# Thresholded attention with a leaky two-layer projection: the weights of period 3 turned by TensorE in five pieces, and a score bank for the second layer of the last group but one

## The chip, the cores and the metric

The kernel runs on one core of a Trainium2 chip. The metric is the device time of one execution in microseconds. Its engines have their own instruction queues and run beside each other: TensorE (PE; its loads of stationary operands are listed as PEld), VectorE (DVE), ScalarE (ACT), GpSimd (POOL), and SyncE (SP), which here mainly issues DMA transfers. TensorE writes only to PSUM, which has eight banks of 2 KB a partition; ScalarE and VectorE take the results out.

## The reference

Eight batches of eight heads, 576 tokens of 64 values each. Every row of scores keeps what lies within tau (0.02) of the row's maximum, takes a softmax over that, and weights v. The result, as 4608 tokens of 512 values, goes through two dense layers with a leaky ReLU between them.

```python
scores = scale * np.matmul(q, k.transpose(0, 1, 3, 2))
thresh = np.max(scores, axis=-1, keepdims=True) - tau
scores = np.where(scores >= thresh, scores, -1000000000.0)
...
attn = np.exp(scores)
attn = attn / (np.sum(attn, axis=-1, keepdims=True) + 1e-09)
return np.matmul(attn, v).astype(np.float32)
...
h = x @ w_in
g = np.maximum(0.01 * h, h)
return (g @ w_out).astype(np.float32)
```

## The kernel before

**Periods.** The work is cut into 72 periods, n = 0 to 71. A main period takes 128 queries of one batch in four heads (two pairs): 8 batches x 4 blocks of queries x 2 halves of the heads. Eight more, the tails, take the last 64 tokens of a batch in all heads. The loop over n (L653) writes the instructions of every engine out by hand in the order in which they are to run; nothing is reordered later. An engine runs its queue in order, and the tile framework puts semaphores where one engine needs another's result or a buffer.

**What one period does.** At step n TensorE computes the scores of period n (L297) into one PSUM tile, `sc`, of five banks (2560 columns). VectorE copies four tiles of 128x576 out of it with their row minima (L338) and derives the thresholds (L356). ScalarE takes exponentials (L367), and VectorE multiplies them with the mask (L378); for the remaining tiles ScalarE does mask and exponential itself (L372, L373). That makes the weights `w` of period n, 128 queries x 18 blocks of 128 keys.

**Turning the weights.** The weighted sum needs the weights with the keys on the partitions. For periods 0 to 2 TensorE turns them against an identity, each block in two halves of 64 columns (`turn_w_here`, L399), into PSUM, and ScalarE or VectorE copies them into `wT` (`take_w`, L404); for periods from 3 on SP issues one DMA that transposes all 18 blocks (`turn_w`, L391), at step n + 1. SP's queue also carries the loads of q, k and v and the stores, in the order of the code.

**Weighted sum and layers.** Two steps later (PV_LAG), TensorE multiplies the turned weights with v (`pv`, L434); VectorE scales the result by the reciprocals of the sums, which TensorE has spread over the partitions (L414) and ScalarE copied to `by` (L420), and writes it to `x` (L453). Two main periods make a group of 128 tokens; its first layer is four pieces (`layer1`, L474, evicted by ScalarE at L477 to `g`), its second layer eight steps (`layer2`, L507), two of them at a time, eight matmuls in all. The result is evicted by ScalarE (L511) and stored by SP. At each step two such pieces of older groups are mixed in, one in each half of the step.

**Loads of the next batch.** q and k are split into halves of 16 bits by POOL, turned by TensorE (`turn`, L186) and copied to `kT` and `qT` (L249). At the first batch and for some pieces of the second, TensorE turns the 32-bit values instead (`turn32`, L211), with ScalarE (L232) and VectorE (L239) taking the two halves out; what `late32` lists for a step is such a piece. POOL loads `w_in` and `w_out` in eight pieces at steps 1 and 4.

**PSUM.** Five banks are `sc`; two more rotate under the tag "h" (turned q and k, turned weights, spread reciprocals, `pv`, the first layer's `hp`); one has the tag "o" (the second layer's sum; at early steps turned weights). The last two periods' `pv`, and the last group's second layer (`layer2_last`, L486), use columns of `sc`, since no scores come after.

Of the kernel before, what the change touches and what calls it, by code (L numbers as in the profile page):

```python
# [9 lines left out]
FP32 = mybir.dt.float32  # L10
FP16 = mybir.dt.float16
# [22 lines left out]
def kernel(  # L34
# [139 lines left out]
    def turn(keys):  # L174

        banks = [ps.tile([128, 1024], FP16, tag="h", bufs=2, name="tp") for _ in range(2)][::-1]
        at_ = 0
        for key in keys:
            half, n = halves.pop(key), tokens(key)
            tps[key] = [t[:, ds(at_, 128 * n)].rearrange("d (x t p) -> d x t p", x=2, t=n) for t in banks]  # L180
            at_ += 128 * n
            for x in range(2):
                for t in range(n):
                    for r in range(2):
                        rows = ds(64 * r, 64)
                        nc.tensor.transpose(tps[key][r][:, x, t, :], half[rows, x, t, :, :].rearrange("p h d -> p (h d)"),  # L186
                                            ident[rows, rows])
        return banks[0]


    def unit32(b, which, p0, np=1, t0=0, nt=4):
# [150 lines left out]
    def copies(st, before, taken, lows):  # L342
        taken()
        if st.n:
            copy_min(st, 1)
            copy_min(st, 2)
        if lows:
            take_low(lows[0])
        if not st.n:
            copy_min(st, 2)  # L350
        copy_min(st, 3)
        for keys in lows[1:]:
            take_low(keys)
        if before:
            recip(before)
        nc.vector.tensor_scalar(out=st.th[:, :], in0=st.mn[:, :], scalar1=1.0, scalar2=tau_f, op0=AX.mult, op1=AX.add)  # L356
        st.w = sb.tile([128, 2, 9, 128], FP16, tag="w", bufs=3, name="w")
        st.sum = sb.tile([128, 2, 2], FP32, tag="sum", bufs=3, name="sum")
# [36 lines left out]
    def turn_w_here(st, first, n, o):  # L395

        for i in range(n):
            for j in range(2):
                nc.tensor.transpose(o[ds(64 * j, 64), ts(i, 128)],  # L399
                                    st.w[:, :, :, :].rearrange("q c n d -> q (c n) d")[:, first + i, ds(64 * j, 64)],  # L400
                                    ident[:, :])

    def take_w(st, first, n, o, copy):
        return copy(out=st.wt[:, :, :, :].rearrange("k c n q -> k (c n) q")[:, ds(first, n), :],  # L404
                    in_=o.rearrange("k (n q) -> k n q", q=128))
# [12 lines left out]
    def take_spread(st, bank):  # L418
        st.by = sb.tile([128, 2, 128], FP16, tag="by", bufs=2, name="by")
        nc.scalar.copy(out=st.by[:, :, :], in_=bank[:, 768:1024].rearrange("d (c q) -> d c q", c=2))  # L420
# [78 lines left out]
    def layer2():  # L499
        g, r = l2q.pop(0)  # L500
        if g.where == (B - 1, 3):
            return layer2_last(g, r)
        if r == 0:
            g.o = ps.tile([128, 512], FP32, tag="o", bufs=1, name="o")
        for j in (2 * r, 2 * r + 1):
            for c in range(2):
                nc.tensor.matmul(out=g.o[ds(64 * c, 64), :], lhsT=g.g[:, j, ds(64 * c, 64)],  # L507
                                 rhs=w_out16[:, j, :], start=(j == 0), stop=(j == 15), skip_group_check=True)
        if r == 7:
            g.out = sb.tile([128, 512], FP32, tag="osb", bufs=3, name="osb")  # L510
            nc.scalar.activation(out=g.out[:, :], in_=g.o[:, :], func=AF.Copy, bias=0.0, scale=1.0)  # L511
            stores.append(g)
# [140 lines left out]
    while n < N + PV_LAG or l1q or pending or l2q or stores:  # L653
        st = periods[n] if n < N else None
        before = periods[n - 1] if 1 <= n <= N else None
        due = periods[n - PV_LAG] if PV_LAG <= n < N + PV_LAG else None
        here = before and before.n < 3
        rest = due and due.n < 3
        plain = 2 if n < 2 or n == 4 else 3
        keys, now32, late = turns_at.get(n, []), early32.get(n, []), late32.get(n)  # L660


        if n == 0:
            def between():
                copy_min(st, 0)
                copy_min(st, 1)
                take_low(k32[1])
                for x in now32:
                    turn32(x)
            scores(st, between)  # L670
            turn32(late)
        elif st:
            scores(st)
        if rest:
            o = ps.tile([128, 1024], FP16, tag="o", bufs=1, name="wp")
            turn_w_here(due, 12, 6, o[:, 0:768])
        bank = turn(keys) if keys else None
        for x in now32 if n else []:
            turn32(x)
        if here:  # L680
            before.wt = sb.tile([128, 2, 9, 128], FP16, tag="wT", bufs=4, name="wT")
            bank = ps.tile([128, 1024], FP16, tag="h", bufs=2, name="tp")
        if due:
            bank = spread(due, bank)
        if here:
            turn_w_here(before, 0, 6, bank[:, 0:768])
        for key in keys:
            take(key, 0, on_act)
        if due:
            take_spread(due, bank)  # L690
        for x in now32:
            take_high(x)
        if here:
            take_w(before, 0, 6, bank[:, 0:768], on_act)
        if st:
            def taken():
                for key in keys:
                    take(key, 1, on_dve)
                if rest:
                    take_w(due, 12, 6, o[:, 0:768], on_dve)  # L700
            copies(st, before, taken, now32)
            exp_plain(st, 0)
            if n == 0:
                exp_plain(st, 1)
                take_high(late)
                take_low(late)
        elif before:
            recip(before)
        work = [lambda key=key: split_pool(key) for key in split_at_.get(n, [])] + pool_at.get(n, [])
        for i, f in enumerate(work):  # L710
            mm = f()
            if i == 0 and before:
                behind_masks(mm, before)
        for key in keys:
            if key[1:] == ("t", "k"):
                widen_keys(key[0])
        if n >= 5:

            for f in small_at.get(n, []):
                f(small=nc.gpsimd)  # L720
        if n < 4:
            idle((4, 10, 8, 4)[n], spare("o"))
        if here:
            o = ps.tile([128, 1024], FP16, tag="o", bufs=1, name="wp")
            if n < 3:
                turn_w_here(before, 6, 6, o[:, 0:768])
        elif before:
            turn_w(before, 1 if st else 2)
        for f in loads_at.get(n, []) + (small_at.get(n, []) if n < 5 else []):
            f()  # L730
        while stores and (n >= N or n not in loads_at or len(stores) > 1):
            store()

        if due and n == 3:
            pv(due)
        if n == 3:
            turn32(late)
            turn_w_here(before, 6, 6, o[:, 0:768])
        for half in range(2):
            if half == 1 and n in (3, 4):  # L740
                exp_steep(st, plain)
            for _ in range(2):
                if l2q:
                    layer2()
            if l1q:
                layer1()
            elif n >= N:
                settle()
            if half == 0:
                if st:  # L750
                    for i in range(1, plain if n else 0):
                        exp_plain(st, i)
                        if n == 3 and i == 1:
                            take_high(late)
                if here:
                    take_w(before, 6, 6, o[:, 0:768], on_act)
                if late and n not in (0, 3):
                    turn32(late)
                    take_high(late)
                if due:  # L760
                    if n != 3:
                        pv(due)
                    evacuate(due)
            elif st and n != 3:
                for i in range(plain + (n == 4), 4):
                    exp_steep(st, i)
        if n == 4:
            take_low(late)
        for i in range(plain if st else 0):
            weights(st, i)  # L770
            if late and n != 4 and n and i == 0:
                take_low(late)
        n += 1
# [33 lines left out]
```

## Time and profile before

| what | value |
|---|---|
| three runs | 477.99, 480.15 and 481.57 us |
| median | 480.15 us |
| profiled execution | 480.22 us |
| its span, first to last instruction | 478.4 us |
| mean granted TensorE clock | 0.996 |
| busy in the span: PE, DVE, ACT, POOL | 462.8, 431.6, 419.1, 216.2 us |
| DMA moved | 84.26 MB, mean 176 GB/s |

A row of the timeline or of the chain begins with the start and the duration in microseconds after the span's start, then engine, line, operation, tiles (out<-in) and how many instructions are merged in it. Brackets at the end give the idle time of the engine before the row and what ended it. Durations of neighbours overlap by some 0.1 us, since the engines pipeline. In the busy time by stretches there follow, after the stretch and its length, the busy time of PE, PEld, DVE, ACT and POOL with their instructions, the granted clock of TensorE, the share of the DMA engines and GB/s. The chain of waits is followed back from the last instruction, at each step to what released it.

### The profile page before, as it was taken

To read this page: it belongs to the slowest core of one execution; us is meant where nothing else is said; L and a number is where in the kernel's file an instruction comes from. 1 tells how busy PE (TensorE), PEld (TensorE's weight loads), DVE (VectorE), ACT (ScalarE), POOL (GpSimd) and SP (SyncE) were. 2 spreads that over 40 slices of the span, in tenths; PEclk is the share of its full clock that TensorE was granted. 3 is DMA by queue.
4 is the path that set the end of the run, shared out by engine and by line. 5 is a ranking of instruction groups with operands and counts; after the bars stand their busy time and mean duration, and the time that the engine had idled before them with its cause. 6 is when DMAs were issued, how large, how long until landed. Compare 5 with 4: busy or idle time off the path is not lost.

```text
span 478.4 us, 25135 instructions
## 1 busy us (share of the span) xinstructions
PE 462.8 (97%) x10806; PEld 377.2 (79%) x10806; DVE 431.6 (90%) x1307; ACT 419.1 (88%) x782; POOL 216.2 (45%) x355
## 2 busy tenths in 40 slices
PE   6889889999999999999999999999999999999997
PEld 4667768888888888888888888888888888877776
DVE  3999969999999999999999999999999999999950
ACT  4898968999999999999999998999999999988862
POOL 2645646554465474455465574545357474000000
PEclk9999989999999999999999999999999999999999
DMA  9999998698899968799889987779889996765561
GB/s 174 236 218 195 188 225 164 156 204 178 201 162 192 246 147 210 117 188 203 186 185 182 210 187 176 150 181 202 189 190 173 200 214 129 117 131 124 123 146 46
DMA packets 208767, 84.26 MB, mean 176 GB/s; under 512 B 177648, under 2 KB 203504, under 8 KB 208656
## 3 DMA queue, kind: packets, MB, share of 16 engines
q1 hardware_dynamic: 201616, 75.25, 79.6%
q0 software_dynamic: 5568, 6.95, 7.7%
q8 instruction: 84, 1.38, 1.2%
q10 hardware_dynamic: 1472, 0.46, 0.4%
q14 instruction: 27, 0.22, 0.2%
HBM read 36.70 MB, written 9.44 MB: 96 GB/s over the span
## 4 chain that ended last, share of the span: by engine, by line
PE 87%; DVE 5%; DMA 4%; ACT 2%; issue 1%; SPq 0%; DVEq 0%; ACTq 0%
PE hp L474 25%; PE o L507 24%; PE sc L297 22%; PE pv L434 8%; DMA wT<-w 3%; PE tp L414 3%; PE tp L186 3%; DVE s L338 3%; DMA raw<-in_k_dram 1%; DVE w L378 1%; PE sc L486 1%; ACT g L477 0%; ACT s L372 0%; SPq L86 0%; ACT e L367 0%
## 5 line engine op out<-in xcount | busy, mean ns | idle before, releaser
L338 DVE TENSOR_SCALAR_CACHE_REDUCE s<-sc 128x576 f32<-128x576 f32 x288 | 205.5, 753 | 18.0 <-PE sc L297 17.9
L474 PEld LDWEIGHTS <-win 128*64 128x64 f16 x4608 | 147.1, 110 | 28.8 <-issue 1.3
L378 DVE SCALAR_TENSOR_TENSOR w<-s,th,e 128x576 f16<-128x576 f32 x213 | 163.6, 815 | 0.2
L367 ACT ACTIVATE e<-s,mn 128x576 f16<-128x576 f32 x213 | 157.8, 778 | 0.0
L507 PE MATMUL o<-wout,g 128*64 128x512 f16 x1120 | 145.0, 380 | 0.6 <-ACT osb L511 0.6
L474 PE MATMUL hp<-x,win 128*64 128x128 f16 x4096 | 137.1, 220 | 0.6 <-DVE x L453 0.3
L477 ACT ACTIVATE g<-hp 128x512 f16<-128x512 f32 x144 | 86.1, 598 | 42.8 <-PE hp L474 42.8
L297 PE MATMUL sc<-kT,qT 64*128 64x384 f16 (+7 forms) x1920 | 120.5, 284 | 2.2 <-DVE s L338 1.3
L297 PEld LDWEIGHTS <-qT 64*128 64x128 f16 (+1 forms) x1920 | 90.7, 97 | 18.6 <-issue 2.2
L160 POOL TENSOR_SCALAR scaled<-raw 128x512 f32<-128x512 f32 x53 | 32.7, 616 | 142.3 <-DVE w L378 129.5
L507 PEld LDWEIGHTS <-g 128*64 128x64 f16 x1120 | 56.8, 110 | 28.5 <-issue 0.7
L171 POOL TENSOR_TENSOR half<-scaled,half 128x512 f16<-128x512 f32 (+1 forms) x68 | 71.7, 1054 | 5.8
L373 ACT ACTIVATE w<-s,minus_tau 128x576 f16<-128x576 f32 x75 | 58.2, 775 | 2.4
L372 ACT ACTIVATE s<-s,th 128x576 f32<-128x576 f32 x75 | 57.5, 767 | 0.7 <-DVE th L356 0.7
L434 PE MATMUL pv<-wT,v 128*64 128x128 f16 (+1 forms) x1560 | 51.6, 214 | 3.7 <-DMA wT<-w 2.7
L434 PEld LDWEIGHTS <-v 128*64 128x64 f16 x1600 | 45.7, 110 | 5.1 <-DMA wT<-w 2.7
L167 POOL CAST half<-scaled 128x512 f16<-128x512 f32 (+1 forms) x68 | 38.3, 563 | 4.4
L453 DVE TENSOR_TENSOR x<-pv,by 128x256 f16<-128x256 f32 x62 | 26.3, 423 | 4.3 <-PE pv L434 4.2
L420 ACT COPY by<-tp 128x256 f16<-128x256 f16 x71 | 26.4, 372 | 0.0
L186 PEld LDWEIGHTS <-half 64*128 64x128 f16 x968 | 24.3, 95 | 2.6 <-issue 1.7
L186 PE MATMUL tp<-ident,half 64*128 64x64 f16 x968 | 24.2, 190 | 0.4 <-issue 0.4
L113 POOL CAST v<-vraw 128x256 f16<-128x256 f32 x64 | 24.5, 417 | 0.0
(64 smaller groups left out, 338.5 us busy)
## 6 DMA issues: line engine op xcount, KB each, us to landing
vraw<-in_v_dram SPq DMA_DIRECT2D x16, 512.0 KB, 5.5
out_dram<-osb SPq DMA_DIRECT2D x31, 256.0 KB, 3.9
raw<-in_q_dram SPq DMA_DIRECT2D x13, 512.0 KB, 4.8
raw<-in_k_dram SPq DMA_DIRECT2D x13, 512.0 KB, 5.5
win<-in_moe_w_in_dram POOLq DMA_DIRECT2D x4, 512.0 KB, 10.6
wout<-in_moe_w_out_dram POOLq DMA_DIRECT2D x4, 512.0 KB, 12.4
raw<-in_q_dram SPq DMA_DIRECT2D x12, 128.0 KB, 3.8
raw<-in_k_dram SPq DMA_DIRECT2D x10, 128.0 KB, 4.4
```

The source lines that it names most:

```text
L171: nc.gpsimd.tensor_tensor(out=halves[key][:, 1, 0:n, :, :], in0=scaled.pop(key)[:, 0:n, :, :], in1=halves[key][:, 0, 0:n, :, :], op=AX.sub ...
L186: nc.tensor.transpose(tps[key][r][:, x, t, :], half[rows, x, t, :, :].rearrange("p h d -> p (h d)"), ident[rows, rows])
L297: yield nc.tensor.matmul(out=o, lhsT=lhs, rhs=turned[st.b, "k"][rows, kx, pair, ds(key0, n)], start=(i == 0), stop=(i == 2), skip_group_ch ...
L338: return nc.vector.tensor_scalar(out=st.s[TILES[n]][:, :], in0=sc[:, ds(PLACE[TILES[n]], 576)], scalar1=-1.0 / UNIT, scalar2=None, op0=AX. ...
L367: nc.scalar.activation(out=st.e[t][:, :], in_=st.s[t][:, :], func=AF.Exp, bias=st.mn[:, n : n + 1], scale=-1.0)
L372: nc.scalar.activation(out=z, in_=z, func=AF.Prelu, bias=st.th[:, n : n + 1], scale=-1.0, alpha=1e20)
L373: nc.scalar.activation(out=w_of(st, t), in_=z, func=AF.Exp, bias=minus_tau[:, :], scale=1.0, accum_out=st.sum[:, c, h : h + 1])
L378: st.last = nc.vector.scalar_tensor_tensor(out=w_of(st, t), in0=st.s[t][:, :], scalar=st.th[:, n : n + 1], in1=st.e[t][:, :], op0=AX.is_le ...
L434: nc.tensor.matmul(out=st.pv[ds(64 * h, 64), c, ts(u, n)], lhsT=v16[st.b % 2][:, pair, blk, :], rhs=st.wt[:, c, blk - (blk > 4), ts(u, n)] ...
L474: nc.tensor.matmul(out=hp[ds(64 * c, 64), jj, :], lhsT=w_in16[:, i, ds(128 * (4 * u + jj) + 64 * c, 64)], rhs=g.x[:, i, :], start=(i == 0) ...
L477: nc.scalar.activation(out=g.g[:, ds(4 * u, 4), :], in_=hp[:, :, :], func=AF.Prelu, bias=0.0, scale=1.0, alpha=0.01)
L507: nc.tensor.matmul(out=g.o[ds(64 * c, 64), :], lhsT=g.g[:, j, ds(64 * c, 64)], rhs=w_out16[:, j, :], start=(j == 0), stop=(j == 15), skip_ ...
```

## The change

Two things are changed. First, the weights of period 3 are turned by TensorE instead of by a DMA from SP, in five pieces of 2, 2, 8, 4 and 2 blocks. At step 4, four blocks go in places that are free in banks already in use ("o" beside the rest of period 2's weights, and the bank of the turned k), and eight in a bank of their own under "o", between the first layer's piece and the late turn of q; at step 5, six go beside the turned q. ScalarE copies three pieces (2, 8 and 2 blocks), VectorE two (2 and 4). At step 4, the late q is turned and its high half copied before, not behind, ScalarE's second exponential. `turn` returns both its banks for this. Second, the second layer of the last group but one, (7, 2), sums in columns 512 to 1024 of `sc` instead of in "o".

```diff
-        return banks[0]
+        return banks
...
-            g.o = ps.tile([128, 512], FP32, tag="o", bufs=1, name="o")
+            g.o = sc[:, 512:1024] if g.where == (B - 1, 2) else ps.tile([128, 512], FP32, tag="o", bufs=1, name="o")
...
-        bank = turn(keys) if keys else None
+        if n == 4:
+            before.wt = sb.tile([128, 2, 9, 128], FP16, tag="wT", bufs=4, name="wT")
+            turn_w_here(before, 0, 2, o[:, 768:1024])
+        bank, side = turn(keys) if keys else (None, None)
...
+        if n == 4:
+            turn_w_here(before, 2, 2, bank[:, 512:768])
+        if n == 5:
+            turn_w_here(due, 12, 4, side[:, 512:1024])
+            turn_w_here(due, 16, 2, bank[:, 512:768])
         if due:
             bank = spread(due, bank)
...
             take_spread(due, bank)
+        if n in (4, 5):
+            take_w(periods[3], (2, 16)[n - 4], 2, bank[:, 512:768], on_act)
...
                 if rest:
                     take_w(due, 12, 6, o[:, 0:768], on_dve)
+                if n == 4:
+                    take_w(before, 0, 2, o[:, 768:1024], on_dve)
+                if n == 5:
+                    take_w(due, 12, 4, side[:, 512:1024], on_dve)
...
-        elif before:
+        elif before and n != 4:
             turn_w(before, 1 if st else 2)
...
             if half == 0:
+                if n == 4:
+                    o = ps.tile([128, 1024], FP16, tag="o", bufs=1, name="wp")
+                    turn_w_here(before, 4, 8, o[:, :])
+                    take_w(before, 4, 8, o[:, :], on_act)
+                    turn32(late)
+                    take_high(late)
...
-                if late and n not in (0, 3):
+                if late and n not in (0, 3, 4):
                     turn32(late)
                     take_high(late)
```

## The prediction

> **What bounds the kernel now.** I read the profile's page first: the clock of TensorE in 40 slices of 12 us, and the chain of work that ended last.
>
> ```profile
> PEclk9999989999999999999999999999999999999999
> ...
> PE 87%; DVE 5%; DMA 4%; ACT 2%; issue 1%; SPq 0%; DVEq 0%; ACTq 0%
> ```
>
> TensorE carries 87% of the chain, so a delay or a gain near the start is mostly carried to the end unchanged. Its clock drops below 9 tenths in one slice, the sixth (59.8 to 71.8 us). I went there with TensorE's timeline, then with the chain in order of time.
>
> ```profile
> 61.50 0.75 PE L434 MATMUL pv<-wT,v 128*64 128x128 f16 x20 [2.42 <-DMA wT<-w]
> ```
>
> ```profile
> 53.09 8.37 DMA wT<-w
> ...
> 62.25 1.19 PE o L507 x8
> 63.43 1.71 PE hp L474 x32
> 65.14 2.05 PE sc L297 x19
> ...
> 71.00 0.86 PE o L507 x8
> 71.87 0.89 PE hp L474 x32
> 72.76 1.65 PE sc L297 x20
> ```
>
> TensorE stands still for 2.42 us (59.08 to 61.50), until the turned weights of period 5 have landed at 53.09 + 8.37 = 61.46. What follows is slow: 1.19 where the same eight matmuls later take 0.86, 1.71 for 0.89, 2.05 for 1.65, together 0.33 + 0.82 + 0.40 = 1.55 us. The busy time by stretches has the reason in the column after the five engines, the granted clock:
>
> ```profile
> 63.00:64.00 1.00, 1.00 (x20) 0.78 (x16) 1.00 (x3) 0.00 (x0) 0.00 (x0) 0.50 1.43 244
> ```
>
> So this stall costs 2.42 + 1.55 = 3.97 us. Why the weights are late stands in SP's queue:
>
> ```profile
> 34.91 3.98 SPq L391 DMA_TRANSPOSE wT<-w  x1
> 39.00 0.50 SPq L75 DMA_DIRECT2D raw<-in_k_dram  x1
> 42.86 7.12 SPq L391 DMA_TRANSPOSE wT<-w  x1
> 50.08 2.90 SPq L86 DMA_DIRECT2D raw<-in_q_dram  x4
> 53.09 3.28 SPq L391 DMA_TRANSPOSE wT<-w  x1
> ```
>
> The three transposes are those of periods 3, 4 and 5, each issued one period later. From 42.86 to 53.09 the queue never rests, so period 5's is issued when SP comes to it. The change takes the first of the three out.
>
> **What periods 4 and 5 pay.** The weights are 18 blocks, so 36 half transposes on TensorE, with copies on ScalarE (256, 1024 and 256 columns) and VectorE (256 and 512). Prices come from turns that exist already: L399 on TensorE (twelve halves in a row of the first fence below) and L404 on ScalarE.
>
> ```profile
> 29.52 0.63 PE L543 MATMUL spare<-blank,ident 128*64 128x256 f16 x8 [0.97 <-DVE wT L404]
> 29.95 0.75 PE L434 MATMUL pv<-wT,v 128*64 128x128 f16 x20
> 30.63 0.65 PE L211 MATMUL tp<-ident,raw 128*128 128x128 f32 x4
> 31.22 0.53 PE L399 MATMUL wp<-ident,w 128*64 128x128 f16 x12
> ```
>
> ```profile
> 36.29 1.08 PE L474 MATMUL hp<-x,win 128*64 128x128 f16 x32 [0.28 <-DVE kT L249]
> ...
> 38.12 0.75 PE L434 MATMUL pv<-wT,v 128*64 128x128 f16 x20 [0.16 <-ACT g L477]
> ```
>
> ```profile
> 32.48 0.79 ACT L404 COPY wT<-wp 128x768 f16<-128x768 f16 x1
> 33.16 0.79 ACT L372 ACTIVATE s<-s,th 128x576 f32<-128x576 f32 x1
> ...
> 36.53 0.38 ACT L420 COPY by<-tp 128x256 f16<-128x256 f16 x1
> ```
>
> Twelve halves take 0.53 us, so one takes 0.044. Period 4 adds 24 of them, 1.06 us. Eight stand ahead of the projection at 36.29; its wait of 0.28 for VectorE swallows 0.17, since only the first four delay what VectorE waits for. The other sixteen stand between that projection and the weighted sum at 38.12, and swallow its wait of 0.16 for ScalarE. That leaves 1.06 - 0.17 - 0.16 = 0.73. Then comes a new wait: the second layer's bank ("o") has held those sixteen halves, and ScalarE copies them out only after it has evicted hp. Its copy of 768 columns runs 0.68 us from start to start (32.48 to 33.16), so 1024 take 0.90. That eviction releases the weighted sum at 38.12 today; behind the new first copy it ends near 38.55, the 1024 columns near 39.45, and TensorE comes for the bank at about the same moment. I put 0.07. Period 4 is 0.80 us later, period 5 another 12 x 0.044 = 0.53. Together 1.33.
>
> ScalarE's side gives the same: 256 columns last 0.38, 0.27 to the next start by the same overlap of 0.11, so its three copies add 0.27 + 0.90 + 0.27 = 1.44, and in period 5 the weighted sum waits for its eviction of hp. The two delays run side by side. VectorE's two copies (some 0.5 us) fall before sums that TensorE brings later still. The late q's turn (L211) keeps its place on TensorE, its copy (L232) goes ahead of the second exponential; VectorE's weighting that needs this one has the copies' delay in hand, so nothing. POOL's queue is unchanged; SP's is passed only by what is taken out. Bounds: 0 if waits hide everything, 1.59 + 1.44 = 3.0 if TensorE's and ScalarE's shares add up. I take 1.33, where the two engines agree.
>
> [...]
>
> **Whether the stall goes.** TensorE will ask for period 5's weights at 59.08 + 1.33 = 60.4. The two ends come from these rows: the time of all 70 transposes on SP's queue (least, median, most, in ns), their median time to landing, and ScalarE's last step of period 5's weights:
>
> ```profile
> L391 SPq DMA_TRANSPOSE wT<-w x70: 1307/2767/7123, 34.9 to 461.6; - x70
> ```
>
> ```profile
> wT<-w SPq DMA_TRANSPOSE x70, 6.0
> ```
>
> ```profile
> 49.63 0.19 ACT L373 ACTIVATION_READ_ACCUMULATOR w<-s,minus_tau 128x1 f32 x1
> ```
>
> Period 4's transpose starts when its weights are ready, 42.86 + 1.4 = 44.25. At worst it holds the queue for 7.12 again, the four loads for 2.90, and period 5's, issued near 54.4, lands 8.37 later at 62.8: a stall as long as today's. With medians the queue is free at 44.25 + 2.77 + 2.90 = 49.9, before the weights of period 5 are ready (49.82 today, so near 51.2); landing is at 57.2, and even with 8.37 at 59.6, in time. I take "in time", because the 7.12 arose behind the k load of 39.00, which now is issued some 4 us earlier.
>
> **The last group but one.** Its second layer no longer waits for the eviction of "o" (L511); it writes into bank 1 of the score tile. In the built instruction stream of the changed kernel that one tile's semaphores take no heed of columns. The group's first matmul waits for the multiply x (L453) of period 70, its second eight for the copy "by" (L420) of period 71, its third eight for x of period 71, and the last group's first L486 for L511. Before the change the second and third eight had no such wait.
>
> ```profile
> 463.89 0.86 PE o L507 x8
> ...
> 465.65 0.56 PE sc L434 x20
> 466.21 0.86 PE o L507 x8
> ```
>
> ```profile
> 461.83 1.05 PE L507 MATMUL o<-wout,g 128*64 128x512 f16 x8 [0.58 <-ACT osb L511]
> ```
>
> ```profile
> 461.36 0.42 DVE L453 TENSOR_TENSOR x<-sc,by 128x256 f16<-128x256 f32 x1
> 466.32 0.42 DVE L453 TENSOR_TENSOR x<-sc,by 128x256 f16<-128x256 f32 x1 [4.53 <-ACT g L477]
> ```
>
> ```profile
> 464.31 0.37 ACT L420 COPY by<-sc 128x256 f16<-128x256 f16 x1
> ...
> 468.87 0.60 ACT L511 ACTIVATE osb<-o 128x512 f32<-128x512 f32 x1 [0.27 <-PE o L507]
> ```
>
> First: x ends at 461.78 and, 0.04 on, the group starts at 461.82 for 461.83, so of the 0.58 only 0.01 is gained. Second: "by" ends at 464.68, so 464.72 for 463.89, 0.83 lost; ScalarE has the eviction of hp ahead of it and can't be sooner. Third: x ends at 466.74, so 466.78 for 466.21, 0.57 more. Fourth: L511 ends at 469.47, while TensorE is in the projection that follows those eight (0.89 from about 468.8): hidden. Sum 1.39 lost. Bounds: -0.58, if only the wait for "o" went, and 1.6, with another 0.1 of wake-up on the two waits.
>
> **Sum.** -3.97 + 1.33 + 1.39 = -1.25 us. The profiled execution took 480.22, of which 478.4 is the span: 479.0. The median of the runs shown is 480.15, which gives 478.9; they reach from 477.99 to 481.57.
>
> **Rivals.** *Slower: the stall stays.* If the backlog is that of w_out's loads and not of the transpose ahead, the landing is the 62.8 worked out: 1.3 later than today, with the same loss of clock, and the tail's 1.39: +2.7, so 482.8. It decides from a landing past 60.4, and outweighs the gain past 61.5. For it: 7.12 is the worst of 70. Against: one whole transpose has gone from ahead of it. Chance 0.14.
>
> *One cost isn't paid*, as periods 4 and 5 hide the turns or the tail's waits are met sooner: -2.6, so 477.5; with both unpaid and 0.58 gained 475.6. Against: TensorE and ScalarE are full there. Chance 0.18.
>
> *The clock drops elsewhere.* [...] Chance 0.06. [...]
>
> **How the numbers follow.** Forecast 0.62; rivals 0.14, 0.18, 0.06. With the runs' own spread the forecast reaches from 477.2 to 480.6. One cost unpaid below, most of the stall above, make it 476.4 to 482.0. One per cent, 4.8 us, is about what a measurement tells from no change. Faster by it needs under 475.35, more than both costs unpaid: 0.05. Slower needs 484.95, the stall kept and the delays in series: 0.06. Within: 0.89.
>
> **What would show it.** Right: no DMA wait near 60, clock 1.00 there, period 5's transpose issued near 51, period 6's scores 1.3 us later, and two L507 near the end idle 0.8 behind L420 and 0.6 behind L453. Wrong: a DMA wait before the weighted sum of period 5 or 6, or those L507 without idle time.

## The result, and the profile after

| | median | lowest to highest | runs | ratio to before |
|---|---|---|---|---|
| before | 480.06 us | 477.36 to 481.91 | 21 | 1 |
| after | 481.85 us | 480.44 to 484.41 | 21 | 1.004 [1.0025, 1.0055] |

The changed kernel is slower by 1.9 us [1.2, 2.6], where 1.25 us less were forecast. The difference is small, but its interval leaves zero out. Here and below a ratio is worked out from the single runs, so it is not the quotient of the two medians, and three of e5's twelve runs, over 1.5% above its fastest, are left out of its ratio. The profiled execution took 480.44 us (span 478.7), the lowest of its 21: one profile beside one profile shows no loss (480.22 to 480.44), and that has to be kept in mind with every row below.

What the forecast said one would see is nearly all there. The page of the changed kernel has no slice with a lower clock, and nearly as much TensorE in the chain of work that ended last (before: 87%):

```profile
PEclk9999999999999999999999999999999999999999
...
q8 instruction: 85, 1.39, 1.2%
...
PE 85%; DVE 5%; ACT 4%; DMA 3%; issue 1%; POOL 0%; DVEq 0%; POOLq 0%; ACTq 0%
```

SP's queue of the changed kernel (start, duration): the k load stands first, period 4's transpose holds the queue for 3.52 us instead of 7.12, and period 5's is issued at 51.48 instead of 53.09.

```profile
31.62 0.37 SPq L75 DMA_DIRECT2D raw<-in_k_dram  x1
44.55 3.52 SPq L391 DMA_TRANSPOSE wT<-w  x1
48.18 2.16 SPq L86 DMA_DIRECT2D raw<-in_q_dram  x4
51.48 3.15 SPq L391 DMA_TRANSPOSE wT<-w  x1
```

TensorE's timeline of the changed kernel has the projection of period 4's step with a wait of 0.18 (before 0.28), the weighted sum behind it with none (0.16), a wait of 0.15 for the bank that held the pieces (0.07 forecast), and at 60.24 the weighted sum that stood still for 2.42 before, without a wait:

```profile
36.69 1.08 PE L474 MATMUL hp<-x,win 128*64 128x128 f16 x32 [0.18 <-DVE kT L249]
...
38.90 0.75 PE L434 MATMUL pv<-wT,v 128*64 128x128 f16 x20
39.80 1.05 PE L507 MATMUL o<-wout,g 128*64 128x512 f16 x8 [0.15 <-ACT wT L404]
...
60.24 0.75 PE L434 MATMUL pv<-wT,v 128*64 128x128 f16 x20
```

At the end of the same timeline stand the two waits of the score bank, 0.84 behind `by` (L420) and 0.58 behind `x` (L453), as the forecast has them, and the 0.58 of the first eight, now behind `x`. The first row was not forecast: the weighted sum of period 70 waits for a transpose.

```profile
458.86 0.75 PE L434 MATMUL sc<-wT,v 128*64 128x128 f16 x20 [0.38 <-DMA wT<-w]
460.20 1.05 PE L507 MATMUL sc<-wout,g 128*64 128x512 f16 x8 [0.58 <-DVE x L453]
...
463.09 1.05 PE L507 MATMUL sc<-wout,g 128*64 128x512 f16 x8 [0.84 <-ACT by L420]
...
466.18 1.05 PE L507 MATMUL sc<-wout,g 128*64 128x512 f16 x8 [0.58 <-DVE x L453]
```

So every mechanism came, and the time did not. To find where it went I cut each profiled execution at starts of scores (the first L297 row of a period in TensorE's timeline). In the kernel before, periods 4 and 9 begin at

```profile
33.10 1.85 PE L297 MATMUL sc<-kT,qT 64*128 64x384 f16 x24
...
72.69 1.61 PE L297 MATMUL sc<-kT,qT 64*128 64x384 f16 x21
```

and 72.69 - 33.10 = 39.59. The three stretches of all profiled executions are below; "loads" is explained further down. (The expectations count the starts with the two of period 0, so their "periods 5 to 10" are periods 4 to 9 here.)

| kernel | period 4 to 9 | 9 to 71 | 71 to the end of the span | TensorE instructions | loads that hit a transpose |
|---|---|---|---|---|---|
| before | 39.59 | 380.18 | 25.52 | 21612 | 24 |
| before, again (e7) | 38.15 | 380.79 | 25.52 | 21612 | 22 |
| e2, bank only | 38.29 | 384.82 | 27.33 | 21612 | 27 |
| e4, no turn of period 3 | 35.08 | 384.58 | 25.60 | 21612 | 25 |
| e5, k load first | 43.07 | 381.52 | 25.58 | 21612 | 24 |
| e6, k and q loads first | 45.30 | 382.60 | 25.57 | 21612 | 23 |
| e12, turn only, fewer spares | 36.44 | 385.02 | 25.64 | 21612 | 23 |
| e10, after, fewer spares | 36.41 | 381.06 | 27.46 | 21612 | 22 |
| e11, no false waits, fewer spares | 36.42 | 385.13 | 26.53 | 21612 | 24 |
| e9, before, more spares | 38.23 | 383.50 | 26.52 | 21684 | 36 |
| after | 36.43 | 380.83 | 28.03 | 21684 | 28 |
| after, again (e8) | 36.41 | 381.89 | 27.97 | 21684 | 27 |
| e1, turn only | 36.42 | 382.64 | 26.44 | 21684 | 34 |
| e3, bank without false waits | 36.41 | 383.57 | 26.36 | 21684 | 32 |

The first and the last column of times repeat to 0.15 us wherever the work and the number of instructions are the same, apart from the stall near 60 us in the kernels that turn period 3 by DMA. The middle one differs by up to 5 us between these executions, and it is no longer where more loads hit (a mean of 382.5 us in the five executions with 21684 instructions, 382.9 in the nine with 21612), so that one profile's middle says nothing about a median.

### The profile page after: what moved, and what is told of

It reads as the page before. It is cut to its first block, busy times and chain, and to the rows that moved or that the text cites. A ratio compares the mean times of both kernels' runs of the same rounds, so it can differ in the third digit from the quotient of the medians.

```text
span 478.7 us, 25209 instructions
## 1 busy us (share of the span) xinstructions
PE 463.6 (97%) x10842; PEld 377.5 (79%) x10842; DVE 431.4 (90%) x1309; ACT 420.3 (88%) x785; POOL 217.3 (45%) x355
## 3 DMA queue, kind: packets, MB, share of 16 engines
q8 instruction: 85, 1.39, 1.2%
## 4 chain that ended last, share of the span: by engine, by line
PE 85%; DVE 5%; ACT 4%; DMA 3%; issue 1%; POOL 0%; DVEq 0%; POOLq 0%; ACTq 0%
PE hp L474 25%; PE o L507 23%; PE sc L297 21%; PE pv L434 8%; DMA wT<-w 3%; PE tp L414 3%; PE tp L186 3%; DVE s L338 2%; DVE w L378 1%; ACT w L373 1%; PE sc L507 1%; PE sc L543 1%; ACT s L372 1%; PE sc L486 1%; ACT e L367 1%
## 5 line engine op out<-in xcount | busy, mean ns | idle before, releaser
L507 PE MATMUL o<-wout,g 128*64 128x512 f16 x1088 | 140.4, 379 | 0.2 <-ACT wT L404 0.2
L297 PE MATMUL sc<-kT,qT 64*128 64x384 f16 (+7 forms) x1920 | 120.2, 284 | 2.7 <-DVE s L338 1.3
L297 PEld LDWEIGHTS <-qT 64*128 64x128 f16 (+1 forms) x1920 | 90.4, 97 | 19.1 <-issue 1.8
L507 PEld LDWEIGHTS <-g 128*64 128x64 f16 x1120 | 56.9, 110 | 30.7 <-issue 2.9
L453 DVE TENSOR_TENSOR x<-pv,by 128x256 f16<-128x256 f32 x62 | 26.3, 424 | 3.4 <-PE pv L434 1.7
L420 ACT COPY by<-tp 128x256 f16<-128x256 f16 x71 | 26.4, 372 | 0.0
```

The lines of the kernel that those rows point to most:

```text
L297: yield nc.tensor.matmul(out=o, lhsT=lhs, rhs=turned[st.b, "k"][rows, kx, pair, ds(key0, n)], start=(i == 0), stop=(i == 2), skip_group_ch ...
```

## First set: the parts one by one

**e1, the turn without the bank.**

```diff
-            g.o = sc[:, 512:1024] if g.where == (B - 1, 2) else ps.tile([128, 512], FP32, tag="o", bufs=1, name="o")
+            g.o = ps.tile([128, 512], FP32, tag="o", bufs=1, name="o")
```

> The first part alone: period 3's weights turned by TensorE, the last group but one back in bank "o". Theory 1 (the stall at period 5's weights is lost in nearly every execution before the change, so its removal is a standing gain, and the score bank spends it at the end): about 2.6 us faster than before, 477.5, ratio 0.994 to 0.996. Theory 2 (that stall is one of several waits for a transpose that come by chance, so that the median gains nothing from the turn, which even adds its 1.3 us): 480 to 481.4, ratio 1.000 to 1.003. The profile of both: no wait for a DMA near 60 us.

Measured: 480.57 against 480.16 us, ratio 0.9995 [0.9973, 1.0017]. The turn by itself changes the time by -0.2 us [-1.3, 0.8]; the forecast had -3.97 + 1.33 = -2.64. So Theory 1 falls; the ratio lies just below Theory 2's range, and its interval overlaps it.

**e2, the bank without the turn** (the kernel before, with the first of the two lines above).

> The second part alone: the score bank, with period 3's weights turned by DMA as before. Both theories: 1.4 to 2.0 us slower than before, 481.5 to 482.1, ratio 1.003 to 1.004, with L507 idle 0.8 us behind L420 and 0.6 us behind L453. A rival to this (the semaphores of the score tile cost nothing in the median, and the loss lies in the first part): no slower than before, ratio 0.999 to 1.001. The profile also gives a second look at period 5's weights: theory 1 has a wait of 2 to 3 us near 60 us again, theory 2 leaves its size open.

Measured: 482.81 us, ratio 1.0057 [1.0034, 1.0079], so 2.7 us [1.6, 3.8], where the forecast had 1.39 and the expectation at most 2.0. Its profiled execution has 1.81 more than the kernel before in the tail (27.33 to 25.52).

**e3, the changed kernel without the false waits**: the second layer of the last group but one is declared to share nothing with the multiplies (L453) and the copies (L420) of the last two periods, which use other columns of the tile.

```diff
+                if g.where == (B - 1, 2):
+                    for x in beside:
+                        tc.declare_no_dep(mm.ins, x.ins, reason="other banks")
```

> Both parts, but the matmuls of the last group but one do not wait for readers of other banks of the score tile (x of periods 70 and 71, by of period 71); the wait for the eviction of "o" stays away too. If those waits are what the second part costs: faster than the changed kernel by 1.8 (the 1.4 predicted plus what the profile showed above it) to 2.4 us, so 479.5 to 480.0; against before, by theory 1 also below it by 2 to 3 us, 477 to 478, by theory 2 level with it. If they are not: 481.9 as the changed kernel.

Measured: 479.80 us, ratio 0.9986 [0.9963, 1.001]. No L507 waits in the tail any more, and 1.7 us of it are gone (28.03 to 26.36). It is still longer than the 25.52 of the kernel before, though the wait for the eviction of "o" is gone as well: two waits for transposes stand there, as in e1, whose tail is 26.44 with the bank "o".

**e4, the turn's cost taken away.** Period 3 uses the turned weights of period 2 and nothing is turned for it, by SP or by TensorE; its rows of the output are therefore others. The bank is "o".

```diff
-            before.wt = sb.tile([128, 2, 9, 128], FP16, tag="wT", bufs=4, name="wT")
-            turn_w_here(before, 0, 2, o[:, 768:1024])
+            before.wt = due.wt
...
-            turn_w_here(before, 2, 2, bank[:, 512:768])
...
-            turn_w_here(due, 12, 4, side[:, 512:1024])
-            turn_w_here(due, 16, 2, bank[:, 512:768])
...
-                    turn_w_here(before, 4, 8, o[:, :])
```

> Period 3's weights are not turned at all: its weighted sum takes period 2's turned weights, so its output is not the reference's; the second part is left out, and the late q keeps its place of the changed kernel. Against the run with the turn alone this prices the five pieces: 1.3 us less by the prediction (periods 5 and 6 begin 0.8 and 1.3 us sooner). Theory 1: 476.2, ratio 0.992. Theory 2: 478.7 to 480, ratio 0.997 to 1.000, since the stall it removes is not there in the median.

Measured: 476.95 us, ratio 0.9945 [0.9923, 0.9968], so -2.6 us [-3.7, -1.5] without the transpose and without the pieces. That lies between the two theories (0.992, and 0.997 to 1.000). In the profiles the pieces are 36.42 - 35.08 = 1.34 us between periods 4 and 9; the forecast had 1.33. That leaves -2.6 + 1.3 = -1.3 for the turn, and e1 measured -0.2. The difference of 1.1 is within the two intervals. If it is real, either the stall is worth less than it looks, or the turn costs something that lies elsewhere.

## Second set: the stall near 60 us

**e7, the kernel before once more**, for a second profile of the stall.

> The kernel before, a second profile. Theory 1, the 3.97 us that the prediction took for the stall are there in every execution: a wait of about 2.4 for period 5's weights and a granted clock of 0.50 for 3.4 us behind it. Theory 2, the wait varies between executions and the drop of the clock is rare (2 of 35 runs of this kernel had a mean clock of 0.996, the others 0.999 or 1.000): a wait of 1 to 3 us for the weights of periods 4 and 5 together, clock 0.999 or 1.000, and the scores of period 10 start 36.4 + 1.3 to 1.9, about 38, us behind those of period 5, not 39.6.

Measured: 480.61 us, mean clock 1.000. Its timeline of TensorE has the stall in another shape:

```profile
49.31 1.05 PE L507 MATMUL o<-wout,g 128*64 128x512 f16 x8 [2.20 <-DMA wout<-in_moe_w_out_dram]
...
62.91 0.75 PE L434 MATMUL pv<-wT,v 128*64 128x128 f16 x20 [0.78 <-DMA wT<-w]
```

2.20 us are now lost to the load of the second half of w_out, and only 0.78 to the weights of period 5. From period 4 to 9 it takes 38.15 us, 3.07 more than e4; e2 has 3.21 more, and the profile that the forecast rested on 4.51. Only the last has the drop of the clock: a mean clock of 0.996 or less, as it had, was there in 2 of 35, 5 of 23 and 7 of 35 runs of the kernel before in the three sets. So Theory 2 holds for the stall: some 3.1 us without the drop, the 1.55 of the drop only now and then.

**e5 and e6, other orders on SP's queue.** The forecast put the late transposes down to the k load of 39.00, which stands ahead of period 4's transpose. If that is it, issuing the loads earlier removes the stall without any work for TensorE. Both are the kernel before with this edit, for n == 4 and for n in (4, 5):

```diff
-        elif before:
+        ahead = n == 4
+        for f in loads_at.get(n, []) if ahead else []:
+            f()
+        if before and not here:
             turn_w(before, 1 if st else 2)
-        for f in loads_at.get(n, []) + (small_at.get(n, []) if n < 5 else []):
+        for f in ([] if ahead else loads_at.get(n, [])) + (small_at.get(n, []) if n < 5 else []):
             f()
```

> The kernel before, with one change of order on SP's queue: in the step of period 4 the k load is issued ahead of period 3's transpose, at about 31.6 us as in the changed kernel, instead of behind it at 39.0. TensorE has no piece of the turn and the bank is 'o'. Theory A, the long occupation (7.12 and 8.13 us in the two profiles that have it) of the queue by period 4's transpose came from the k load's traffic beside it: it falls to some 3.5 to 4, period 5's transpose is issued near 50, the waits for period 4's and 5's weights go, and the time is that of the kernel without any turn of period 3, ratio near 0.995 (477.0 to 478.0). Theory B, it comes from period 3's own transpose being in flight: 7 to 8 us as before, the waits stay, ratio 1.000 within 0.002.

> As the run with the k load ahead, and in the step of period 5 the four q loads go ahead of period 4's transpose too. If their buffer is free by then they are issued near 39 and period 5's transpose is issued as soon as its weights are ready (49 to 51) whatever period 4's takes; then by theory A the ratio is that of the run before or a little better (0.993 to 0.996), by theory B the wait for period 5's weights goes while that for period 4's stays, ratio 0.996 to 0.999. If their buffer is not free, period 4's transpose is issued late, and the time grows by as much: a wait of 2 us or more for period 4's weights, ratio over 1.003.

Measured: e5 483.76 us, ratio 1.0054 [1.0029, 1.0080]; e6 485.65 us, ratio 1.0117 [1.0082, 1.0152]. Both are slower, which neither theory had for e5. In e5 the transposes of periods 3 and 4 hold SP's queue for 18.69 us together, and TensorE's timeline has a wait of 4.63 for the weights of period 3, with the clock at 0.50 for 6.83 us from 1.4 us before the end of that wait on:

```profile
34.54 18.69 SPq L391 DMA_TRANSPOSE wT<-w  x2
```

```profile
50.16 1.28 PE L434 MATMUL pv<-wT,v 128*64 128x128 f16 x20 [4.63 <-DMA wT<-w]
```

Its DMA issues between 28 and 56 us took, from issue to landing (median, us):

```profile
wout<-in_moe_w_out_dram POOLq DMA_DIRECT2D x2, 512.0 KB, 14.8
...
wT<-w SPq DMA_TRANSPOSE x2, 14.7
```

where the changed kernel, in the same window, has

```profile
wout<-in_moe_w_out_dram POOLq DMA_DIRECT2D x2, 512.0 KB, 8.1
...
wT<-w SPq DMA_TRANSPOSE x2, 6.5
```

In e6 the same wait is 4.75; its ratio is that of the expectation's last case, but the wait is for period 3's weights and not for period 4's. With the k load in front, period 3's transpose is in flight beside that load and the second half of w_out, and lands late itself. Which of the two makes it late was not tested. But the late weights near 60 us are not put right by moving the k load alone. All six profiles that turn period 3 by DMA have such waits, each its own: for period 3's weights (e5, e6), period 4's and 5's (e2, 0.28 and 1.73), w_out and period 4's (e9, 0.94 and 1.81), w_out and period 5's (e7), or period 5's alone (before). All eight profiles without that transpose have none between 30 and 72 us. Of what was tried, only one transfer less takes the waits away, which is what the change does. By theory B, too, the k load's place is not the cause; its figures for e5 were wrong all the same.

**e8, the changed kernel once more.**

> The changed kernel again, beside these runs. Ratio 1.002 to 1.0055 as before, so 0.9 to 2.7 us more than the kernel before. In the profile the same two waits of the last group but one, 0.8 behind by (L420) and 0.6 behind x (L453), no wait for a DMA near 60 us, periods 5 to 10 in 36.4 us; what lies between period 10 and the tail varies by 1 to 4 us with chance waits for transposes.

Measured: 482.14 us, ratio 1.0042 [1.0017, 1.0067], as in the first comparison. Periods 4 to 9 take 36.41, the tail 27.97: both as before, to 0.1 us. So the wait for a transpose at the weighted sum of period 70 is no chance: it stands in all four profiles with the pieces so far (after, e8, e1 and e3: 0.38, 0.38, 0.42, 0.45), and in none of the six without them.

## Third set: what 72 instructions do

The page lists packets of a queue q8 of kind "instruction". In the trace they are 16384 bytes each, 84 of them in the kernel before and 85 after; with 21612 and 21684 TensorE instructions (a matmul counts two, its weight load and itself), that is about one per 256. I take them for loads of TensorE's program. What one of them does to a transpose is seen in the bytes moved, 13 us around the start of period 71's scores, in 40 slices of 0.325 us (the bytes of a packet count in the slice where it starts). Before:

```profile
GB/s 214 218 221 220 213 157 54 0 0 0 0 0 0 0 0 122 217 207 218 216 217 221 217 248 158 183 252 151 38 19 58 220 210 209 179 215 215 217 195 326
...
wT<-w SPq DMA_TRANSPOSE x4, 4.2
```

After:

```profile
GB/s 219 217 216 213 212 170 52 0 0 0 0 0 0 0 0 122 218 209 208 217 217 266 167 9 5 9 35 360 385 227 57 209 161 16 117 284 281 224 239 291
...
wT<-w SPq DMA_TRANSPOSE x4, 5.5
```

The zeros of the first half are the gap between two pairs of transposes, in both. Then, in the middle of a transpose, the changed kernel has four slices in which all DMA engines together move 5 to 35 GB/s, and the median landing goes from 4.2 to 5.5 us. A load of 16384 bytes starts at 456.18, 0.4 us ahead of the hole, 5.52 behind the start of period 71's scores. In the kernel before, the same load comes 6.25 behind that start, when the transpose is through. The transpose that is hit is the one TensorE waits for, by the chain of waits of the changed kernel:

```profile
452.96 5.86 DMA wT<-w
```

Over the whole trace, a load "hits" if within 1.6 us behind it at least eight packets of SP's queue of up to 1 KB, nearly all of them of transposes, take more than 1 us each (the median of such packets is 0.018). The last column of the table has the counts: 22 to 27 in the nine executions with 21612 instructions, 27 to 36 in the five with 21684. That such packets belong to the loads shows in their places: in the kernel before, 438 of the 496 packets of 256 bytes that took more than 1 us start within 1.6 us behind a load, and after the change 490 of 557, though these stretches are only some 28% of the span. So the theory (F in the expectations): the 72 instructions of the pieces shift all later loads by 72 of 256 instructions, and onto transposes that are needed soon. The test is to add 72 instructions that do nothing, and to take 72 away.

**e9, the kernel before with 72 more.** Of the blank matmuls that fill the waits of the first 22 us (L543), 36 are split into two of half the width.

```diff
-                nc.tensor.matmul(out=bank[ds(64 * c, 64), 0:256], lhsT=ident[:, ds(64 * c, 64)], rhs=blank[:, :],
-                                 start=True, stop=True, skip_group_check=True)
+                for x in ((0, 128), (128, 128)) if i < halves else ((0, 256),):
+                    nc.tensor.matmul(out=bank[ds(64 * c, 64), ds(*x)], lhsT=ident[:, ds(64 * c, 64)], rhs=blank[:, ds(*x)],
+                                     start=True, stop=True, skip_group_check=True)
```

> The kernel before with 36 of the 84 blank matmuls of the first 22 us (L543) split into two of half the width: 72 TensorE instructions more, as many as the change adds, at the same work. Theory F: TensorE's instructions are loaded 16384 bytes (256 rows) at a time, a load that meets a DMA transpose delays it by over 1 us, and the 72 added rows shift which transposes are met. Then the load that comes 6.3 us behind the start of period 71's scores comes at 5.6, as in the four kernels with the pieces, the weighted sums of periods 70 and 71 wait 0.4 to 0.5 each, the tail from those scores to the end of the span is 26.4 instead of 25.5, and the ratio is 1.001 to 1.004. Theory N, the wait in the tail has to do with the pieces themselves: tail 25.5, ratio 1.000 within 0.0015.

Measured: 483.80 against 481.44 us, ratio 1.0052 [1.0029, 1.0075]: 2.5 us [1.4, 3.6] more, for nothing that TensorE computes. Period 4 begins at 33.25 (33.10 and 34.35 in the two profiles of the kernel before), so nothing shows that the added matmuls cost time where they stand. The load comes 5.62 behind the start of period 71's scores, the hole is there,

```profile
GB/s 212 216 211 273 130 4 3 9 10 234 0 0 0 0 0 121 217 209 210 216 219 271 206 74 4 9 9 297 378 208 53 186 185 25 167 264 261 213 47 0
...
wT<-w SPq DMA_TRANSPOSE x4, 5.6
```

and so are the waits of the weighted sums of periods 70 and 71 in TensorE's timeline:

```profile
463.17 0.75 PE L434 MATMUL sc<-wT,v 128*64 128x128 f16 x20 [0.37 <-DMA wT<-w]
...
468.80 0.47 PE L434 MATMUL sc<-wT,v 128*64 128x128 f16 x10 [0.47 <-DMA wT<-w]
```

The tail is 26.52 (expected 26.4). Theory F is shown for the tail. The whole cost is larger than the tail's 1.0, so the rest lies between; that loads which hit there cost it (36 against 24 over the whole trace) is argued, not shown.

**e10, e11, e12: 72 fewer.** In each, 36 of the blank matmuls replace 72, at twice the width; they then have as many TensorE instructions as the kernel before. e10 is the changed kernel, e11 is e3 and e12 is e1.

```diff
-        for i in range(k):
+        for i in range(k - doubles):
+            wide = 512 if i < doubles else 256
             for c in range(2):
-                nc.tensor.matmul(out=bank[ds(64 * c, 64), 0:256], lhsT=ident[:, ds(64 * c, 64)], rhs=blank[:, :],
+                nc.tensor.matmul(out=bank[ds(64 * c, 64), 0:wide], lhsT=ident[:, ds(64 * c, 64)], rhs=blank[:, 0:wide],
```

> The changed kernel with 36 blank matmuls fewer, by making 36 of them twice as wide in place of 72: as many TensorE instructions as the kernel before. Theory F: the loads fall as before the change, no wait for a DMA in the tail, which is 27.3 (25.5 and the 1.8 of the score bank) instead of 28.0; ratio 1.000 to 1.0025. Theory N: as the changed kernel, tail 28.0, ratio 1.004.

> The changed kernel without the false waits of the score tile and with 36 blank matmuls fewer. Theory F: tail 24.9 (25.5 less the 0.6 that the first eight matmuls of L507 waited for the eviction of 'o') instead of 26.4; ratio 0.994 to 0.997, faster than both kernels. Theory N: as without the change of the blank matmuls, tail 26.4, ratio 0.9986.

> The turn alone (bank 'o') with 36 blank matmuls fewer. Theory F: periods 5 to 10 in 36.4 as with the turn alone, tail 25.5 instead of 26.4; the turn's own gain of 1.8 (38.2 less 36.4) is then left standing, ratio 0.995 to 0.998. Theory N: as the turn alone, tail 26.4, ratio 0.9995.

Measured:

| | median (before 481.44) | ratio | the same without the edit | tail |
|---|---|---|---|---|
| e10 | 481.39 us | 1.0008 [0.9980, 1.0036] | 1.0040 [1.0025, 1.0055] | 27.46 (28.03) |
| e11 | 481.11 us | 0.9992 [0.9963, 1.0021] | 0.9986 [0.9963, 1.0010] | 26.53 (26.36) |
| e12 | 480.09 us | 0.9963 [0.9936, 0.9990] | 0.9995 [0.9973, 1.0017] | 25.64 (26.44) |

e10 and e12 come out as Theory F has them: no wait for a transpose in the tail, which e12 has as the kernel before (25.64 to 25.52), and 1.5 us less in both ratios, though each of these two differences by itself has an interval of about 1.6 to either side. They also compare ratios from two chips, each taken beside the kernel before on the same chip; e9 needs no such step. With the phase of the loads as it was, the turn alone is faster than the kernel before by 1.8 us [0.5, 3.1], as the stretch from period 4 to 9 says (38.15 - 36.44 = 1.7). Its ratio is below those of both kernels and is the lowest of the versions that compute the reference; against e3 and e11 the intervals overlap. e11 misses: its tail has a wait for the weights of period 71.

```profile
468.74 0.47 PE L438 MATMUL sc<-wT,v 128*64 128x128 f16 x10 [1.49 <-DMA wT<-w]
```

Its last transpose lands 4.89 us after its issue, where e10's takes 3.26. Without the false waits TensorE runs ahead in the tail, so the next load, too, comes earlier, 11.66 behind the start of period 71's scores (before 12.30), as the last packets of that transpose go out. No packet there takes more than 1 us, so by the count above this load hits nothing; a few packets trail on until the landing. That the load is the reason is read from one profile; no run takes it away.

## Why the prediction was wrong

**What held.** The stall near 60 us and the drop of the clock went, and period 5's transpose was issued at 51.48 (near 51 was said). The pieces cost 1.34 us (1.33), and period 6's scores begin 15.79 us behind period 4's instead of 14.45, so 1.34 later (1.3). The waits of the score bank are 0.84 and 0.58 (0.83 and 0.57), behind the instructions that were named. Nor did the clock drop elsewhere: no slice of the page is below 9 tenths, and from 33 to 48 us, where the 36 half transposes are added, every microsecond of the changed kernel was at 1.00.

**The step that failed: the sum puts what 72 more TensorE instructions do outside of periods 4 and 5 at nothing.** Its three terms are the stall, the pieces and the bank, on the ground that "a delay or a gain near the start is mostly carried to the end unchanged". With the count of instructions as before (e12) the gain does come through to the end, with the 72 it doesn't. The forecast counted the 36 half transposes by their time alone. That they are 72 instructions, and shift the loads of TensorE's program against the transposes of the other 66 periods, was not looked at, although the page lists the queue. The runs put 1.5 us (e1 to e12), 1.5 (after to e10) and 2.5 (e9) on it; e3 to e11 shows nothing (-0.3). Weighted by their intervals that is about 1.7 us [0.9, 2.4], more than the whole gain that was forecast.

**Two sizes were off besides.** The stall's -3.97 was read from one execution, which had the rare drop of the clock. Against e4, e7 and e2 have 3.07 and 3.21, and e4 itself gives -2.6 [-3.7, -1.5] in the median. The reason given for it fell, too: "the 7.12 arose behind the k load of 39.00" is what e5 tried, and it got worse.

The tail's 1.39 is 1.82, in the difference of e10 and e12 (27.46 - 25.64) and in that of e2 and the kernel before. TensorE's timeline has the reason. Before, from the spread of the reciprocals and from the weighted sum to the second layer:

```profile
463.59 0.30 PE L414 MATMUL sc<-ident,rec 128*64 128x128 f16 x4
463.70 1.06 PE L507 MATMUL o<-wout,g 128*64 128x512 f16 x8
...
465.46 0.75 PE L434 MATMUL sc<-wT,v 128*64 128x128 f16 x20
466.01 1.06 PE L507 MATMUL o<-wout,g 128*64 128x512 f16 x8
```

And in e10:

```profile
461.66 0.30 PE L414 MATMUL sc<-ident,rec 128*64 128x128 f16 x4
462.80 1.05 PE L507 MATMUL sc<-wout,g 128*64 128x512 f16 x8 [0.84 <-ACT by L420]
...
464.55 0.75 PE L434 MATMUL sc<-wT,v 128*64 128x128 f16 x20
465.89 1.05 PE L507 MATMUL sc<-wout,g 128*64 128x512 f16 x8 [0.59 <-DVE x L453]
```

From start to start it is 0.11 before and 1.14 in e10, then 0.55 and 1.34: 1.03 + 0.79 = 1.82. The waits are 0.84 + 0.59 = 1.43 of it; the other 0.39 is the overlap that is lost, as a matmul that doesn't wait starts some 0.2 us before the one ahead of it is through (463.70 against 463.89, 466.01 against 466.21 in the rows of before). The forecast took its starts from the chain of waits (463.89 where the timeline has 463.70), and the chain puts a start behind the end of the work before it.

**The sum as it should have been**: -3.1 (stall) + 1.3 (pieces) + 1.8 (bank) + 1.7 (loads) = +1.7 us; measured 1.9 [1.2, 2.6]. The single parts fit as well: e12 -3.1 + 1.3 = -1.8 (measured -1.8), e10 0.0 (0.4), e2 1.8 (2.7 [1.6, 3.8]); e1 would be -0.1 (-0.2). The 1.7 was drawn in part from the changed kernel and e1 themselves, so their sums are no test of it; those of e12, e10 and e2 do without it.

**What stays open.** How the 1.7 us divide over the 62 periods between was not settled: of the tail there is 0.57 (after and e10), 0.80 (e1 and e12) and 1.00 (e9 and before), the rest is only the difference to the medians, and no profile shows it. Only 72 instructions were added or taken away; another count would shift the loads to other places, and what it costs or gains there is not known. And if e11 is read rightly, the phase cannot be set for the whole program by a count alone, since a load's place depends on what TensorE waits for, too.

## What to carry to other kernels

A gain read from one execution is that execution's: look whether the thing to be removed (a drop of the clock, a wait for one transfer of many) is there in a second profile before giving it its full price. Added instructions had a price beside their time here, about 1.7 us for 72, as the loads of 16384 bytes came at other places among the kernel's critical transfers; a null edit of the same count (here 36 blank matmuls split in two) measures it, and belongs beside every change of a few microseconds that adds or removes many instructions. The waits at the end cost their idle time and the overlap with the work ahead (1.82 us for 1.43 of idle time); take the starts from an engine's timeline.

## What the runs showed of the hardware

**In the tail, a transpose nearly stood still behind a load of instructions.** One packet of 16384 bytes took 0.9 to 1.6 us around the tail, and in the transposes that were hit there 16 to 22 packets took up to 1.4 to 1.9 us, with the bytes moved by all DMA engines together down from above 200 to between 2 and 10 GB/s for about 1 us. The trace does not tell the engines apart, but a total of 2 to 10 GB/s leaves hardly any of them starting new packets. No run here shows why they stand still.

**The clock's drop did not go by the length of the wait alone.** In the kernel before, a wait of 2.42 us was followed by 3.41 us at a granted clock of 0.50, from 1.16 us after its end on, and in e11 (mean clock 0.996) one of 2.08 near 286 us by as much, from 0.10 us after; in e7 (mean clock 1.000) one of 2.20 was followed by none. In e5, with a wait of 4.63 us, 6.83 us, twice as long, were at 0.50, which is the slice with 7 tenths on its page:

```profile
PEclk9999799999999999999999999999999999999999
```

What sets the length of a drop, and why one wait of some 2 us has it and another has not, no run here shows.
